# Equal column tiles for the scores, a planner that prices TensorE's tiling, masks on a second engine, and a due time for each attention step

## The chip, the cores and the metric

The kernel runs on one core of one Trainium2 chip. The metric is the device time of one execution in microseconds (us), the median of several runs. The profile is of one execution; its own time is given beside its span below.

The engines in this text: PE is TensorE (matmuls; PEld its weight loads), DVE is VectorE, ACT is ScalarE, POOL is GpSimd, and SP is the engine whose queue issues every DMA of this program.

## The reference

```python
# q, k, v: 4 batches x 8 heads x 768 positions x 64, float32; n_global = 8, n_local = 96
scores = q @ k.T / sqrt(64)
is_global = key < n_global
is_local  = 0 <= query - key < n_local
bias = -slope[head] * distance          # ALiBi; n_local for global keys out of the local window
scores = where(is_global | is_local, scores + bias, -1e9)
a = exp(scores - max);  a = a / (sum(a) + 1e-9);  y = a @ v
x = y, heads side by side               # 3072 tokens x 512
out = ((x @ w_a) * (x @ w_b)) @ w_out   # 512 -> 1536 -> 512
```

So: attention over a window of 96 keys and 8 global ones, and behind it a gated feed-forward layer on the same 3072 tokens. The weights are float64 and reach the device as pairs of 32-bit words.

## The kernel before

**Tiling.** The tokens are cut into six *sequences* u of 512 tokens (four blocks of 128). Names carry the numbers: `ps2_0_1_0` is sequence 2, granule 0, step 1, half 0.

**Attention.** A sequence is four *granules* p; a granule holds four pairs of block and head pair, that is 4 x 128 queries x 2 heads. Its chain:

1. *Scores* (L581, PE, into banks ps): two steps of two blocks each, 48 steps in the program. The array works as four tiles of 64x64: the head (h) picks the rows, the half of the queries (s) picks the columns of the array. A query half needs 168 keys: 96 near ones and 8 global ones, which stand side by side (KX = 104), and 64 more, which lie elsewhere for the lower half (s = 0) and directly behind for the upper half.
2. *Mask* (L602, DVE): one instruction per block and head adds the mask, takes the minimum and writes `t` in SBUF and its row minimum in `sm`. The masks themselves (L514) are made once, one 336-column instruction per head.
3. *Exponential* with row sum (L619, ACT), reciprocal (DVE), *norm* (L658 on ACT or L661 on DVE).
4. *Transposes*: in sequence 0 on PE (`direct`, L749, into banks pt, copied out into px and py); else on DVE (L677, into tt), and through DRAM (`mir`) back into px and py (`carry`, DMAs of SP).
5. *Values* (L701, PE, bank pa): 16 matmuls, then a copy of pa into `X`. In sequences 1 to 3 the values of a granule are emitted after the scores of the next.

**Feed-forward.** The 1536 hidden units are six weight tiles `fp`, each a pair of 128-unit halves for both w_a and w_b and two tiles O0, O1 of w_out. A weight tile is loaded (wr, 512 KB pieces), *converted* from float64 (L369 and L404 on ACT, L376, L384, L394, L411 on DVE) and split into a high and a low part in fp32r, so each product of two numbers takes three matmuls. `STAYS` says which tiles stay for which sequences: tiles 0 to 2 for sequences 0 to 3 with plain products (L943), later stays with a seven-product form (L922). Products go into the banks al and ga, ACT and DVE make h = a * b and its two parts hh and hl, and output matmuls (L1099) add into acc0 to acc3. A stay leaves partial sums in DRAM (part) for the next.

In sequence 0 the tokens are done in two halves of 256, named `(0,)` and `(1,)`: `al0_2_1(1,)` is sequence 0, tile 2, hidden half 1, token half 1.

**What sets the order.** Nothing is reordered on the chip: each engine runs its instructions as written. `Schedule.order` writes them. Every operation is given a due time, a cost on each engine that may do it, and what it reads and writes; the planner simulates the engines with these costs, and whenever one is free it takes, of the operations whose inputs are ready and whose buffers are free, the one that is due first. `wins` decides for operations that two engines may do. The due times come from tables at the head of the file: HALF0, HALF1, STEPS0, QUADS0 to QUADS2 and GAP for sequence 0, SPANS for the attention of sequences 1 to 5 (as positions in the list of passes), CONV for the conversion of tiles. All operations of a granule's chain have one due time, `due`; values and their copy have `due + VLAG`. The core of the planner's choice:

```python
for item in ready[e]:
    op = item[2]
    if e in op.port and port > now:
        continue
    if fits(op) and wins(op, e):
        break
...
free[e] = now + op.costs[e]
```

## Time and profile before

| | before |
|---|---|
| time, median of 3 runs (lowest to highest) | 725.11 us (724.22 to 725.52) |
| the profiled execution: its time, its span | 728.68 us, 726.4 us |
| granted TensorE clock, mean | 0.987 |
| busy in the span: PE, DVE, ACT | 693.5, 578.9, 387.7 us |

The profile is read in stretches: the attention of sequence 0 (7 to 62 us, in which the first weight tiles are converted and the first products begin), its feed-forward (62 to 128 us), sequences 1 to 3 with the first stay (to about 300 us), and the later stays, in which attention of sequences 4 and 5 lies among the products. "PEclk" is the clock that the throttle granted, as a share of full speed. In the rows of the order of time a bracket names the idle time ahead of an instruction on its engine, and what ended it. A row of such a view begins with the start in us and the busy time in us; where rows are grouped, "xcount" and "busy, mean ns" follow. L-numbers are lines of the kernel before; in the rows of the changed kernel the same operations stand some 20 to 26 lines further down (L581 is L607, L602 L628, L619 L645, L701 L727, L943 L969, L1099 L1125, L369 L391, L332 L354).

### The profile page before, as it was taken

The page shows a single profiled execution, that of the slowest core. Times are in us where ns is not written, and L with a number is a line of the kernel's source. Part 1 is how long each engine was busy: PE and PEld are TensorE (multiplying, and loading weights), DVE is VectorE, ACT ScalarE, POOL GpSimd, SP SyncE. Part 2 cuts the span into 40 slices and gives each one's busy share as a digit, 9 for nine tenths or more (in the row PEclk, how much of TensorE's full clock was granted, in tenths as well). Part 3 has the DMA queues.
Part 4 walks back from the last instruction along what each step waited for, and adds up shares of the span by engine and source line. Part 5 has one row for each costly group of instructions (what it writes and reads, how often), then busy time and mean ns, then how long its engine had stood idle before and what let it go on. Part 6 is the DMA issues. An engine that isn't in the chain of part 4 may idle for free.

```text
span 726.4 us, 15134 instructions
## 1 busy us (share of the span) xinstructions
PE 693.5 (95%) x5584; PEld 605.8 (83%) x5584; DVE 578.9 (80%) x1544; ACT 387.7 (53%) x989; POOL 1.8 (0%) x8
## 2 busy tenths in 40 slices
PE   5698998999999999999999999999999999999996
PEld 4487887777777788788899899899989999999995
DVE  7999997777687785799989898999999557746652
ACT  5987775745465673746455545666343434434310
POOL 1000000000000000000000000000000000000000
PEclk9799999999999999999999999999999999999999
DMA  8547998897989897776676888756794423343221
GB/s 296 213 163 259 269 294 300 267 305 250 304 280 303 253 335 247 262 266 228 221 249 232 294 259 301 245 201 230 233 337 151 146 59 102 131 145 102 74 73 62
DMA packets 67906, 162.39 MB, mean 224 GB/s; under 512 B 8432, under 2 KB 21872, under 8 KB 66032
## 3 DMA queue, kind: packets, MB, share of 16 engines
q1 hardware_dynamic: 67824, 161.34, 66.8%
q8 instruction: 46, 0.75, 0.4%
q14 instruction: 36, 0.29, 0.1%
HBM read 110.45 MB, written 50.86 MB: 222 GB/s over the span
## 4 chain that ended last, share of the span: by engine, by line
PE 68%; DMA 12%; DVE 11%; ACT 5%; issue 2%; SPq 1%; DVEq 0%; ACTq 0%
PE acc L1099 19%; PE al L922 16%; PE ga L922 12%; DMA wr<-wts 8%; PE ps L581 4%; PE pa L701 3%; ACT t L619 1%; DMA py<-mir 1%; DVE tt L677 1%; DMA X<-dx 1%; DVE t L602 1%; DVE wm L394 1%; ACT wm L369 1%; DVE wm L411 1%; SPq L323 1%
## 5 line engine op out<-in xcount | busy, mean ns | idle before, releaser
L1099 PE MATMUL acc<-w_O,hh 128*128 128x512 f32 x576 | 196.6, 400 | 0.0
L1099 PEld LDWEIGHTS acc<-w_O,hh 128*128 128x128 f32 x576 | 108.4, 188 | 25.1 <-issue 1.7
L1099 PE MATMUL acc<-w_O,hl 128*128 128x512 f32 x288 | 113.8, 395 | 0.4 <-DVE hl L342 0.3
L619 ACT ACTIVATE t<-t,sm 128x168 f32<-128x168 f32 x192 | 81.1, 424 | 20.2 <-DVE sm L602 20.0
L922 PE MATMUL al<-xf_T,w_S 128*128 128x256 f32 x576 | 76.8, 283 | 0.0
L922 PEld LDWEIGHTS al<-xf_T,w_S 128*128 128x128 f32 x576 | 72.2, 189 | 0.5
L332 ACT CAST hh<-h 128x512 fp32r<-128x512 f32 (+1 forms) x62 | 36.6, 592 | 50.2 <-DVE h L342 22.5
L1099 PEld LDWEIGHTS acc<-w_O,hl 128*128 128x128 f32 x288 | 54.3, 188 | 10.5 <-DVE hl L342 1.1
L581 PEld LDWEIGHTS ps<-qk 64*64 64x64 f32 x1152 | 36.3, 142 | 28.1 <-issue 14.2
L602 DVE CUSTOM_DVE_ANT_0 t<-ps,mask 128x168 f32<-128x168 f32 x192 | 53.3, 326 | 6.1 <-PE ps L581 5.6
L581 PE MATMUL ps<-qk 64*64 64x168 f32 (+2 forms) x1152 | 43.6, 278 | 14.4 <-DMA qk<-qk 7.0
L332 ACT COPY s<-al 128x512 f32<-128x512 f32 x47 | 27.5, 585 | 52.2 <-PE al L922 52.2
L369 ACT ACTIVATE wm<-wr 128x512 f32<-128x512 f32 x54 | 36.2, 670 | 34.7 <-DMA wr<-wts 25.2
L342 DVE TENSOR_TENSOR hl<-h,hh 128x512 fp32r<-128x512 f32 (+1 forms) x78 | 49.8, 642 | 5.2 <-ACT hh L332 4.9
L1031 DVE TENSOR_TENSOR s<-ga,s 128x512 f32<-128x512 f32 x48 | 32.8, 683 | 16.2 <-PE ga L922 16.0
L677 DVE STREAM_TRANSPOSE tt<-t 128x512 f32<-128x512 f32 x80 | 41.1, 552 | 0.8 <-ACT t L658 0.4
L404 ACT ACTIVATE wr<-wr 128x512 int32<-128x512 uint32 x54 | 36.2, 673 | 7.2 <-DMA wr<-wts 4.3
L701 PE MATMUL pa<-px,vt 104*64 104x128 f32 x384 | 38.9, 278 | 1.2 <-DMA px<-mir 1.2
L922 PE MATMUL ga<-xf_B,w_S 128*128 128x256 f32 x288 | 38.6, 283 | 1.3 <-ACT s L332 1.3
L922 PEld LDWEIGHTS al<-xf_B,w_A 128*128 128x128 f32 x288 | 37.5, 189 | 2.3 <-issue 0.3
L922 PE MATMUL ga<-xf_T,w_S 128*128 128x256 f32 x288 | 38.6, 283 | 0.6 <-DVE s L1031 0.5
L701 PE MATMUL pa<-py,vt 128*64 128x128 f32 x384 | 38.0, 273 | 1.1 <-DMA py<-mir 1.0
(274 smaller groups left out, 1318.6 us busy)
## 6 DMA issues: line engine op xcount, KB each, us to landing
wr<-wts SPq DMA_DIRECT2D x54, 512.0 KB
qk<-qk SPq DMA_DIRECT2D x24, 720.0 KB
mir<-tt SPq DMA_DIRECT2D x20, 768.0 KB
vt<-vd SPq DMA_DIRECT2D x24, 512.0 KB
X<-dx SPq DMA_DIRECT2D x10, 1024.0 KB
part<-o SPq DMA_DIRECT2D x32, 256.0 KB
wl_S<-dw_S SPq DMA_DIRECT2D x32, 256.0 KB
px<-mir SPq DMA_DIRECT2D x60, 128.0 KB
```

Source lines behind the costliest of these rows:

```text
L332: self.nc.scalar.copy(out(), src())
L342: lambda e: self.nc.vector.tensor_tensor(out(), a(), b(), op=op),
L369: lambda e: nc.scalar.activation(m(), high().bitcast(F32), AF.Abs),
L404: lambda e: nc.scalar.activation(low(), low().bitcast(U32), AF.Copy, scale=2.0**-29),
L581: nc.tensor.matmul(ps[h][64 * s : 64 * s + 64, c0 + c : c0 + c + w], qk[rows, q0 + 64 * s : q0 + 64 * s + 64], qk[rows, k0 + k : k0 + k + ...
L602: nc.vector.tensor_tensor_reduce(t[:, i, h], b[:, w], self.mask[pair][:, h, kind], -0.125, 3.0e38, ALU.add, ALU.min, sm[:, 0, j : j + 1],)
L619: lambda e, i=i, h=h, j=j: nc.scalar.activation(t[:, i, h], t[:, i, h], AF.Exp, bias=sm[:, 0, j : j + 1], scale=-1.0, accum_out=sm[:, 1, j ...
L677: nc.vector.transpose(dst[:, :, e0 : e0 + n], src[:, :, c0 : c0 + 32 * n].rearrange("p j (e k) -> p j e k", e=n),)
L701: nc.tensor.matmul(pa[64 * h : 64 * h + 64, i * P : i * P + P], vt[:lanes, v0 : v0 + 64], k[:, :, 2 * i + h], start=c == 0, stop=c == 1, s ...
L922: self.nc.tensor.matmul(bank[:, ab * HT : ab * HT + HT], w[:, a, (2 * ab + c) * P : (2 * ab + c) * P + P], x[:, b, c], start=first, stop=F ...
L1031: lambda e: nc.vector.tensor_tensor(s[:, :], bank[:, :], s[:, :], op=ALU.add),
L1099: self.nc.tensor.matmul(acc[i][:, :], a[:, rows], w[:, b], start=first and f == 0 and k == 0, stop=False, skip_group_check=True,)
```

## The change

1. **Score tiles.** Both query halves take their 168 columns as 104 and 64. Before, the upper half took 168 at once. A step goes from 12 to 16 matmuls.
2. **The planner.** An operation on PE can carry a mode; scores and values have mode "t" (tiled). A change of mode is charged SWITCH = 250 ns, and if the operation due first would change it, the planner looks for one of the present mode that is due at most KEEP = 1500 ns later. Costs of scores go from 720 to 620 ns, of values from 1900 to 1760.
3. **Masks** may be made on ACT.
4. **Due times.** Each step of a granule has its own offset: LEAN for sequence 0, LEAN1 for the others (scores, mask, exponential, norm, transposes, values in sequence 0 or the way through DRAM in the others; the seventh of LEAN is the copy into X). Scores are due 2.31 us earlier in sequence 0 and 0.9 us earlier elsewhere; in sequence 0 values are due 5.0 and their copy 5.64 us behind the granule's time.
5. **Tables.** Of the numbers at the head of the file FORM0 (a lead of the first forms of X), LOADLEAD (lead of the loads of q and k), HALF0, HALF1, GAP, one to three entries of STEPS0 and QUADS0 to 2, the end of SPANS[2], the start of SPANS[5] and the start of CONV[5] change.

```diff
-SPANS = {1: (0.0, 0.6), 2: (0.85, 1.6), 3: (1.6, 2.6), 4: (3, 7), 5: (6.79, 11.5)}
+SPANS = {1: (0.0, 0.6), 2: (0.85, 1.3), 3: (1.6, 2.6), 4: (3, 7), 5: (6.7, 11.5)}
-CONV = {3: (1.72, 2.88), 4: (2.5, 3.5), 5: (4.39, 7), 2: (7.27, 10), 0: (10, 12.27), 1: (11.39, 14)}
+CONV = {3: (1.72, 2.88), 4: (2.5, 3.5), 5: (4.14, 7), 2: (7.27, 10), 0: (10, 12.27), 1: (11.39, 14)}
...
+KEEP = 1500.0
+SWITCH = 250.0
+LEAN = (-2310.0, 0.0, 0.0, 0.0, 0.0, 5000.0, 5640.0)
+LEAN1 = (-900.0, 0.0, 0.0, 0.0, 310.0, 0.0)
...
+                    cost = op.costs[e]
+                    if e == "pe":
+                        if op.mode != mode:
+                            for other in ready[e]:
+                                if other[0] > op.due + KEEP:
+                                    break
+                                if other[2].mode == mode and fits(other[2]):
+                                    item, op = other, other[2]
+                                    break
+                        cost = op.costs[e] + (SWITCH if op.mode != mode else 0.0)
+                        mode = op.mode
...
+TILES = [(s, h, 0, 64, KX) for s in range(2) for h in range(2)]
+TILES += [(s, h, KX, (0, KW)[s], 64) for s in range(2) for h in range(2)]
...
+        def scale(e, out, hd):
+            by = self.slope[:, hd : hd + 1]
+            if e == "act":
+                nc.scalar.mul(out, rel(), by)
+            else:
+                nc.vector.tensor_scalar(out, rel(), by, None, op0=ALU.mult)
...
-                    for s, c, k, w in ((1, 0, 64, KW), (0, 0, 64, KX), (0, KX, 0, 64)):
-                        for h in range(2):
...
+                    for s, h, c, k, w in TILES:
...
-            op(due, scores, [qk], ps, pe=720)
+            op(due + lean[0], scores, [qk], ps, pe=620).mode = "t"
```

What the new due times and costs do to the order is seen only in the built programs. Four places follow.

**ACT at the start**, up to the conversion of the first weight pieces. Before:

```order
L1476 TENSOR_LOAD flag_76
L1479 COMPARE_AND_BRANCH
L619 ACT_TABLE_LOAD
L619 ACTIVATE t0_0_160,sm0_0_161<-t0_0_160,sm0_0_161 128x168 x8
L369 ACTIVATE wm0_1_224<-wr0_1_152 128x512
L404 ACTIVATE wr0_1_152<-wr0_1_152 128x512
```

With the change:

```order
L1502 TENSOR_LOAD flag_76
L1505 COMPARE_AND_BRANCH
L535 ACT_TABLE_LOAD
L535 ACTIVATE mask0_162<-X_81,slope_80 128x336
L535 ACTIVATE mask1_165<-X_81,slope_80 128x336
L535 ACTIVATE mask2_172<-X_81,slope_80 128x336
L645 ACTIVATE t0_0_168,sm0_0_169<-t0_0_168,sm0_0_169 128x168 x8
L391 ACTIVATE wm0_1_242<-wr0_1_160 128x512
```

Three masks now stand ahead of the first eight exponentials; DVE makes the other five.

**PE in sequence 0, second token half**, where products fill the banks al and ga. Before:

```order
L943 MATMUL al0_0_1(1,)_900<-xp0_2_458,w0_A22_0_456 128x256 x3
L943 MATMUL al0_0_1(1,)_900<-xp0_3_482,w0_A22_0_456 128x256 x3
L943 MATMUL al0_1_0(0,)_932<-xp0_0_361,w1_A11_0_740 128x256 x3
L943 MATMUL al0_1_0(0,)_932<-xp0_1_372,w1_A11_0_740 128x256 x3
L943 MATMUL al0_1_0(0,)_932<-xp0_2_458,w1_A12_0_773 128x256 x3
L943 MATMUL al0_1_0(0,)_932<-xp0_3_482,w1_A12_0_773 128x256 x3
L943 MATMUL al0_1_1(0,)_959<-xp0_0_361,w1_A21_0_852 128x256 x3
```

With the change:

```order
L969 MATMUL al0_0_1(1,)_950<-xp0_2_481,w0_A22_0_476 128x256 x3
L969 MATMUL al0_0_1(1,)_950<-xp0_3_521,w0_A22_0_476 128x256 x3
L969 MATMUL ga0_0_1(1,)_973<-xp0_0_361,w0_A21_0_443 128x256 x3
L969 MATMUL ga0_0_1(1,)_973<-xp0_1_469,w0_A21_0_443 128x256 x3
L969 MATMUL ga0_0_1(1,)_973<-xp0_2_481,w0_A22_0_476 128x256 x3
L969 MATMUL ga0_0_1(1,)_973<-xp0_3_521,w0_A22_0_476 128x256 x3
L969 MATMUL al0_1_0(0,)_993<-xp0_0_361,w1_A11_0_758 128x256 x3
```

A product into ga now lies between two into al; in all of sequence 0 an al product follows another directly once, and three times before.

**ACT at the end of sequence 0** (wm3: conversion of weight tile 3; X from pa1_3: the copy of the last values of sequence 1; xp1: the forms of X for sequence 1; o0: output sums of sequence 0 on their way out; hh: high parts of h). Before:

```order
L369 ACTIVATE wm3_0_1619<-wr3_0_1582 128x512
L332 CAST xp1_0_1626<-X_81 128x512
L332 CAST xp1_2_1636<-X_81 128x512
L332 COPY o0_0_87371_1644<-acc0_0_704 128x512
L332 COPY o0_1_87371_1650<-acc0_1_713 128x512
L404 ACTIVATE wr3_0_1582<-wr3_0_1582 128x512
L332 COPY o0_2_87371_1667<-acc0_2_1022 128x512
L369 ACTIVATE wm3_1_1692<-wr3_1_1648 128x512
L332 COPY X_81<-pa1_3_1670 128x512
```

With the change:

```order
L354 COPY o0_1_99841_1700<-acc0_1_747 128x512
L426 ACTIVATE wr3_0_1643<-wr3_0_1643 128x512
L354 CAST xp1_0_1710<-X_81 128x512
L354 CAST xp1_2_1718<-X_81 128x512
L354 CAST hh0_2_1_1630<-h0_2_1_1612 128x256
L354 COPY X_81<-pa1_3_1722 128x512
L391 ACTIVATE wm3_1_1752<-wr3_1_1704 128x512
L354 CAST xp1_3_1772<-X_81 128x512
L354 COPY o0_2_99841_1775<-acc0_2_1040 128x512
```

The copy into X stands ahead of the conversion of wr3_1 now, and the form xp1_3 behind it.

**PE at the values of granule 2 of sequence 2** (bank pa2_2). Before:

```order
L943 MATMUL ga1_2_1(0, 1)_2301<-xp1_3_1702,w2_A22_0_1407 128x512 x3
L1099 MATMUL acc1_0_2061<-w1_O0_0_1092,hh1_1_0_1984 128x512
L1099 MATMUL acc1_0_2061<-w1_O0_0_1092,hl1_1_0_1989 128x512
L1099 MATMUL acc1_0_2061<-w1_O0_0_1092,hh1_1_0_1984 128x512
L701 MATMUL pa2_2_2335<-px0_248,vt2_2_2059 64x128 x2
L701 MATMUL pa2_2_2335<-py0_133,vt2_2_2059 64x128 x2
```

With the change:

```order
L969 MATMUL ga1_2_1(0, 1)_2413<-xp1_3_1772,w2_A22_0_1490 128x512 x3
L727 MATMUL pa2_2_2435<-px0_261,vt2_2_2148 64x128 x2
L727 MATMUL pa2_2_2435<-py0_137,vt2_2_2148 64x128 x2
L727 MATMUL pa2_2_2435<-px0_261,vt2_2_2148 64x128 x2
L727 MATMUL pa2_2_2435<-py0_137,vt2_2_2148 64x128 x2
L727 MATMUL pa2_2_2435<-px0_261,vt2_2_2148 64x128 x2
```

Three output matmuls into acc1_0, which stood ahead of these values, now stand behind them.

On DVE, in sequences 1 to 3, conversions of weights come earlier and attention's transposes later than before. The runs of tiled matmuls on PE, between products and output matmuls, number 63 before and 64 with the change.

More of the change, by code (lines that the diff above doesn't have):

```diff
@@ L83 @@
 AHEAD = 0.5
-FORM0 = 2410.0
+FORM0 = 3520.0
 START = 25980.0
-LOADLEAD = 7790.0
+LOADLEAD = 8130.0
 VLAG = 13280.0
@@ L174, in op @@
         self.ops.append(Op(len(self.ops), due, costs, emit, reads, writes, late, port))
+        return self.ops[-1]
     def order(self):
@@ L185, in order @@
         port = 0.0
+        mode = None
         def arrive(op):
@@ L240, in order @@
                     out.append(op)
-                    free[e] = now + op.costs[e]
+                    free[e] = now + cost
                     if e in op.port:
@@ L513, in masks @@
                 -1e5 + hd if p < 2 else 4000.0 + hd,
-                lambda e, p=p, h=h, hd=hd: nc.vector.tensor_scalar(
-                    self.mask[p][:, h].rearrange("p a b -> p (a b)"),
-                    rel(),
-                    self.slope[:, hd : hd + 1],
-                    None,
-                    op0=ALU.mult,
+                lambda e, p=p, h=h, hd=hd: scale(
+                    e, self.mask[p][:, h].rearrange("p a b -> p (a b)"), hd
                 ),
@@ L524, in masks @@
                 dve=dve(n, True),
+                act=act(n),
             )
@@ L680, in turn @@
                     )
-            op(due, turn, ts, [(tt, half)], dve=dve(512) + dve(256))
+            op(due + lean[4], turn, ts, [(tt, half)], dve=dve(512) + dve(256))
         if u not in DIRECT:
-            self.carry(n, due, tt, px, py)
+            self.carry(n, due + lean[5], tt, px, py)
         def late():
-            self.values(u, p, due, vt, px, py, x, d)
+            self.values(u, p, due + (VLAG if u else lean[5]), vt, px, py, x, d)
         return late
@@ L713, in values @@
         pr += [(py, ("b", i, s)) for i in range(NH) for s in range(2)]
-        op(due + VLAG, values, [vt] + pr, [pa], pe=1900)
+        op(due, values, [vt] + pr, [pa], pe=1760).mode = "t"
         if d is None:
@@ L717, in values @@
                 self.copy(
-                    due + VLAG, lambda: x[:, p], lambda: pa[:, :], T, [pa], halves(x, p), psum=True
+                    due, lambda: x[:, p], lambda: pa[:, :], T, [pa], halves(x, p), psum=True
                 )
@@ L731, in values @@
             return
-        self.copy(due + VLAG, lambda: vt[:, :T], lambda: pa[:, :], T, [pa], [vt], psum=True)
+        self.copy(due, lambda: vt[:, :T], lambda: pa[:, :], T, [pa], [vt], psum=True)
         self.dma(
-            due + VLAG,
+            due,
             lambda: d[:, p * T : p * T + T],
```

50 lines of the change are left out of this document (26 added, 24 removed).

## The prediction

> **What bounds the kernel now.** I read the page's first lines, then the busy times by stretch (each row: the stretch, its length, each engine's busy time, the granted clock, the DMA share), then the chain and the order of time where PE stands idle.
>
> ```profile
> span 726.4 us, 15134 instructions
> PE 693.5 (95%) x5584; PEld 605.8 (83%) x5584; DVE 578.9 (80%) x1544; ACT 387.7 (53%) x989; POOL 1.8 (0%) x8
> ...
> core 0: us, PE busy (x) PEld busy (x) DVE busy (x) ACT busy (x) POOL busy (x), PEclk, DMA share, GB/s
> 0.00:7.00 7.00, 0.00 (x0) 0.00 (x0) 2.33 (x11) 1.28 (x1) 1.83 (x8) 1.00 0.61 196
> 7.00:20.00 13.00, 10.94 (x168) 9.42 (x168) 12.93 (x62) 9.79 (x36) 0.00 (x0) 1.00 0.87 315
> 20.00:38.00 18.00, 11.45 (x121) 9.35 (x116) 17.48 (x72) 17.36 (x63) 0.00 (x0) 0.73 0.57 215
> 38.00:62.00 24.00, 20.60 (x223) 17.72 (x222) 22.57 (x80) 20.30 (x63) 0.00 (x0) 0.93 0.63 212
> 62.00:118.00 56.00, 54.24 (x530) 48.35 (x530) 52.12 (x173) 39.40 (x113) 0.00 (x0) 0.99 0.85 269
> 118.00:128.00 10.00, 8.02 (x71) 6.02 (x70) 6.70 (x22) 4.58 (x13) 0.00 (x0) 0.83 0.96 343
> 128.00:300.00 172.00, 170.12 (x1296) 133.84 (x1295) 126.46 (x383) 99.18 (x274) 0.00 (x0) 1.00 0.85 283
> 300.00:550.00 250.00, 248.00 (x2041) 224.02 (x2040) 231.50 (x554) 137.96 (x329) 0.00 (x0) 1.00 0.75 250
> ```
>
> PE bounds the program. Its idle time is 32.9 us: 7.0 before the first scores, 12.0 from 7 to 62 us, 1.8 to 118, 2.0 to 128, 1.9 to 300, 2.0 to 550, and 6.2 behind that, almost all at the end. From 7 to 62 us it is DVE that has no time left (53.0 of 55 us), and PE waits for it. So the change can gain little after 62 us, 7.6 us of idle time at the very most, unless PE's own work shrinks.
>
> **Masks on ScalarE.** DVE made four masks before the first scores could be read; now two of them and one later one stand on ACT.
>
> ```profile
> 8.44 1.31 DVE L514 TENSOR_SCALAR mask<-X,slope 128x336 f32<-128x336 f32 x4
> 9.66 0.33 DVE L602 CUSTOM_DVE_ANT_0 t<-ps,mask 128x168 f32<-128x168 f32 x1
> 10.03 0.43 ACT L619 ACTIVATE t<-t,sm 128x168 f32<-128x168 f32 x1 [3.11 <-DVE sm L602]
> 23.64 0.42 PE L749 MATMUL pt<-ident,t 128*104 128x128 f32 x1 [3.47 <-DVE t L661]
> ```
>
> Four masks took 9.66 - 8.44 = 1.22 us, 0.30 each, so three are worth 0.9 us of DVE. ACT was idle for 3.11 us there, which hides them: a 336-column operation on ACT is not in the trace; between its 168 columns (0.43) and, without a limit from above, twice that (0.86), three end between 9.8 and 11.1 us, and the first exponential moves by -0.2 to +1.1 us. I take 0.45 each, nearest the lower row. Behind this, two granules' exponentials and norms keep their order, and PE's 3.47 us wait at 23.64 stays, about 0.5 us sooner. In return the plan puts five evictions of transposes more on DVE by 45 us, and the forms that gate the first product come no sooner. Price: -0.4, between -0.9 and +0.5.
>
> **Products alternate between the banks.** In sequence 0 each half-product (12 matmuls of 256 columns) fills bank al or ga. Three times one al product follows another directly and waits for ACT to copy the bank out.
>
> ```profile
> 64.88 1.68 PE L943 MATMUL al_1(1,)_900<-xp,w_A 128*128 128x256 f32 x12
> 67.02 1.68 PE L943 MATMUL al_0(0,)_932<-xp,w_A 128*128 128x256 f32 x12 [0.46 <-ACT s_1(1,)_918 L332]
> 69.20 1.69 PE L943 MATMUL al_1(0,)_959<-xp,w_A 128*128 128x256 f32 x12 [0.50 <-ACT s_0(0,)_955 L332]
> ...
> 102.68 1.59 PE L943 MATMUL ga_1(0,)_1461<-xp,w_A 128*128 128x256 f32 x12
> 104.10 1.58 PE L943 MATMUL al_0(1,)_1489<-xp,w_A 128*128 128x256 f32 x12
> 106.14 1.69 PE L943 MATMUL al_1(1,)_1524<-xp,w_A 128*128 128x256 f32 x12 [0.46 <-ACT s_0(1,)_1519 L332]
> ```
>
> Without a wait starts lie 104.10 - 102.68 = 1.42 apart; with it 2.14, 2.18 and 2.04, so 0.6 to 0.8 us each. The new order has one such pair (al0_1_1 before al0_1_0 of the other half). Two fewer: -1.4, between 0 (something later is the limit) and -2.1.
>
> **The end of sequence 0.** Before, the copy of the last values (X) stands on ACT behind a weight conversion whose DMA is late; the scores behind it on PE wait for the bank.
>
> ```profile
> 119.31 0.44 PE L701 MATMUL pa<-py,vt 128*64 128x128 f32 x4 [0.24 <-DMA py<-mir]
> 121.00 0.50 PE L581 MATMUL ps<-qk 64*64 64x168 f32 x2
> 123.24 0.81 PE L581 MATMUL ps<-qk 64*64 64x168 f32 x22 [1.74 <-ACT X L332]
> ...
> 122.05 0.66 ACT L369 ACTIVATE wm<-wr 128x512 f32<-128x512 f32 x1 [3.42 <-DMA wr<-wts]
> 122.61 0.57 ACT L332 COPY X<-pa 128x512 f32<-128x512 f32 x1
> ...
> 124.05 4.55 PE al_0(0, 1)_1726 L943 x12
> 139.80 2.80 PE al_0(0, 1)_1899 L943 x12
> 583.95 5.60 PE acc L1099 x24
> ...
> 177.58 0.44 PE L701 MATMUL pa<-px,vt 104*64 104x128 f32 x4 [1.16 <-DMA px<-mir]
> ```
>
> The new order has the copy ahead of the conversion, so the scores no longer wait: 123.24 - 121.00 = 2.2 us. It also moves two groups of three output matmuls (6 of 5.60 / 24 = 0.23 us, 1.4 us) behind the values; that much PE then waits in front of them, since the values are held by the DMA of py anyway (119.31). Net 0.8 us. One form, xp1_3, is still cast behind the conversion; its product starts with the other three, which take 2.1 us, and I cost it at nothing. If the weight DMA comes over 2 us later, al1_0_0 stalls instead. Then the clock: behind the 2.2 us wait the next product took 4.55 us against 2.80 for an equal one, and PEclk reads 0.83 there, while after the wait of 1.16 at 177.58 the stretch's PEclk stays at 1.00. With the wait cut to some 1.4 us, most of those 1.75 us should return: I take 1.4. Together -2.2, between 0 and -3.9 (2.2 + 1.75). The Trainium skill ("TensorE: Matmul & The Clock Gate", Part 1) says that the array goes to half clock after an idle window of about 3.4 us; by it this 2.2 us gap would have cost no clock, and the term would be 0.8. The trace differs, so its rows decide.
>
> **The values of granule 2, sequence 2.** At 177.58 they already wait for the way through DRAM. The new order puts three output matmuls behind them that stood ahead: 3 x 0.23 = +0.7, between 0 (the DMA comes sooner) and +1.5 (it comes that much later).
>
> **Tilings and matmuls.** The plan now charges 250 ns for a change of tiling and looks for an equal one, yet the built order has 64 runs of tiled matmuls, 63 before.
>
> ```profile
> 150.12 2.99 PE ga_1(0, 1)_2017 L943 x12
> ...
> 153.04 0.82 PE L581 MATMUL ps<-qk 64*64 64x168 f32 x24
> 153.79 0.50 PE L1099 MATMUL acc<-w_O,hh 128*128 128x512 f32 x1
> ...
> L1099 PE MATMUL acc<-w_O,hh 128*128 128x512 f32 x576 | 196.6, 400 | 0.0
> ```
>
> A product before a run takes 2.99 instead of 2.80, and the first matmul behind it 0.50 instead of its group's mean of 0.40: 0.3 us a run, so +0.3 (0 to 0.6). Each of the 48 scores steps goes from 12 to 16 matmuls, 24 to 32 records. The streamed columns stay. Lower tile columns already did 104 + 64, the upper ones 168, side by side, and the step took 153.79 - 153.04 = 0.75 for the longer of the two; with both as 104 + 64 I take 0. Bounds: -0.5 in all (10 ns a step), and from above the records in proportion, 0.25 us a step, 12 us.
>
> **The rest**, dues of attention and of the conversion of tiles 4 and 5, moves work among DVE, ACT and SP from 128 to 550 us, where PE idles 3.9 us in all: I take 0, between -2 and the loss below. The last 164 us before 714 keep their order of products.
>
> **Sum:** -0.4 - 1.4 - 2.2 + 0.7 + 0.3 = -3.0. The profiled execution took 728.68 us (2.28 outside the span), 3.57 over the median of 725.11; 728.68 less 3.0 is 725.68, and that less 3.57 is 722.1.
>
> **Rivals.** *Conversions ahead of attention.* In sequences 1 to 3 the new DVE order does weight conversions earlier and attention's transposes later. Ahead of the transposes of granule 1, sequence 3, stand one more piece of a tile's conversion (four operations) and the four combining operations of tile 4, each the size of L394's.
>
> ```profile
> L394 DVE SCALAR_TENSOR_TENSOR wm<-wr,wm 128x512 int32<-128x512 int32 x54 | 36.9, 684 | 0.7
> L411 DVE CUSTOM_DVE_ANT_0 wm<-wr,wm 128x1024 uint16<-128x1024 uint16 x54 | 36.8, 682 | 0.8
> ...
> L384 DVE TENSOR_SCALAR wm<-wm 128x512 int32<-128x512 int32 x54 | 22.7, 420 | 0.5
> L376 DVE TENSOR_SCALAR wm<-wm 128x512 f32<-128x512 f32 x54 | 22.5, 417 | 15.0 <-ACT wm L369 12.6 <-DMA py<-mir 2.4
> ...
> 250.18 1.71 SPq L323 DMA_DIRECT2D py<-mir  x4
> ...
> 254.09 0.44 PE L701 MATMUL pa<-px,vt 104*64 104x128 f32 x4
> ```
>
> A piece is 0.68 + 0.68 + 0.42 + 0.42 = 2.2 us, the four others 4 x 0.68 = 2.7: 4.9 us more ahead. DVE idles 45 us from 128 to 300, which should take this in. But the way from transpose to values has no slack: the last load of granule 3, sequence 3, is issued by 251.9, and PE starts those values 2.2 us later. If the idle time lies elsewhere, the 4.9 us become waits of PE in front of values: 722.1 + 4.9 = 727.0. It turns slower once they come over 4.5 us late. *Small matmuls cost.* If a record held its tile quarter for the mean 0.75 / 24 = 31 ns beside its columns, the four more records of the upper quarters would make 0.125 us a step, 6.0 in all: 728.1. Against it: the halves with more records set no longer time that I can see. The Trainium skill ("TensorEngine Tiling (Array Packing)", Instruction Overhead) states about 60 cycles for each matmul; by it, 25 ns, it would be 4.8 us and 726.9. *The gains turn into waits.* DVE and DMA (85% busy from 62 to 118) hand over at the same time as before, PE reaches the values of sequence 1 earlier and waits longer there, the clock falls again: only -0.4 + 0.7 + 0.3 stay, and -0.8: 724.9. *The charge does nothing* is already counted: the runs are not fewer.
>
> **Numbers.** My forecast 0.50 (719 to 724), gains turned into waits 0.22, conversions ahead 0.20, small matmuls 0.08. A change under 0.2% (1.45 us) is about what a measurement of this kernel cannot tell from none. Faster, below 723.66: nearly all of the first and little of the second, 0.52; within: 0.25; slower: 0.23. The range goes from all lower bounds of the three gains (-6.9, less 0.7 and 0.3 of loss, and 1.7 of the 3.9 us idle behind 128 us: 725.1 - 7.6 = 717.5) to the dearest rival, 728.5.
>
> **What the profile after would show.** First exponential by 10.2 us; one al product with a wait for ACT between 60 and 110 us instead of three; the scores of sequence 2 without a wait for X, and the first product of the second pass at 2.8 to 3 us; a wait of 2 us at the values of granule 2; scores steps still 0.75 us. Wrong would make it: scores steps over 0.78, waits for px or py over 2 us in sequences 2 and 3, or ACT held at a weight DMA with a form behind it.

## The result, and the profile after

The changed kernel took 733.39 us in the median of 4 runs (730.75 to 737.24), the kernel before 725.32 in 4 runs beside them: a ratio of 1.0115, with a 95% interval from 1.0075 to 1.0156. It is slower, by about 8 us. The profiled execution took 731.67 us.

The first lines of its profile, and the busy times by stretch:

```profile
span 730.2 us, 15911 instructions
PE 693.6 (95%) x5968; PEld 605.2 (83%) x5968; DVE 576.4 (79%) x1546; ACT 389.5 (53%) x987; POOL 1.8 (0%) x8
...
62.00:118.00 56.00, 53.64 (x590) 47.80 (x590) 50.86 (x170) 38.58 (x109) 0.00 (x0) 1.00 0.88 279
118.00:128.00 10.00, 9.85 (x111) 7.42 (x106) 9.58 (x35) 7.41 (x23) 0.00 (x0) 1.00 0.98 311
128.00:300.00 172.00, 169.30 (x1431) 132.84 (x1430) 131.80 (x402) 97.22 (x263) 0.00 (x0) 1.00 0.88 291
300.00:550.00 250.00, 243.52 (x2086) 220.02 (x2086) 221.39 (x529) 136.50 (x323) 0.00 (x0) 1.00 0.74 244
```

The 384 more instructions of PE are the 48 x 8 more records of the scores. PE is as busy as before (693.6 against 693.5 us). From 118 to 128 us it now idles 0.15 us instead of 2.0; from 128 to 300 it idles 2.7 instead of 1.9, and from 300 to 550 6.5 instead of 2.0.

The profiled execution before was 3.6 us over the median. The better yardstick is a control that ran later: the order and tiles of before, put out from a list, in a program that is the same instruction by instruction. Its traced execution took 723.59 us:

```profile
span 721.4 us, 15134 instructions
...
128.00:300.00 172.00, 171.82 (x1304) 135.40 (x1303) 130.66 (x398) 104.00 (x290) 0.00 (x0) 1.00 0.87 286
300.00:550.00 250.00, 248.95 (x2040) 226.26 (x2040) 231.73 (x548) 135.11 (x317) 0.00 (x0) 1.00 0.75 250
```

There PE idles 0.2 and 1.05 us, 1.2 from 128 to 550 us; the changed kernel idles 9.2 in the same stretches. These 8.0 us come near the difference of the two spans (8.8), but only because the rest nearly cancels: up to 128 us the changed kernel idles 3.8 us less than the control, behind 550 us 0.6 more, and PE is busy 4.0 us longer in all (693.6 against 689.6). What PE waited for there, first in the changed kernel from 128 to 300 us and from 300 to 550 (us in total, times, longest):

```profile
PE pa L727 <- DMA px<-mir: 1.1, 2, 0.8
PE pa L727 <- DMA py<-mir: 0.9, 2, 0.5
PE ps L607 <- ACT X L354: 0.4, 1, 0.4
...
PE ga L948 <- DVE s L1057: 2.2, 3, 1.8
PE ga L948 <- ACT s L354: 1.3, 1, 1.3
PE pa L727 <- DMA px<-mir: 1.3, 1, 1.3
PE pa L727 <- DMA py<-mir: 0.8, 1, 0.8
PE al L948 <- ACT s L354: 0.8, 1, 0.8
```

Values that wait for their way through DRAM (px, py) make 4.1 us, products that wait until DVE or ACT has read their bank out (s) 4.3, scores that wait for X 0.4. In the control the same view has one wait of 0.2 from 128 to 300 and three, 0.8 together, behind that. The second kind shows in the order of time how a queue passes a delay on (DVE, the changed kernel; then the product that waits, on PE):

```profile
545.94 0.69 DVE L1160 TENSOR_TENSOR o<-acc,o 128x512 f32<-128x512 f32 x1 [1.26 <-DMA o<-part]
546.55 0.42 DVE L356 CAST xf_B<-X 128x512 fp32r<-128x512 f32 x1
547.00 0.69 DVE L364 TENSOR_TENSOR xf_B<-X,xf_B 128x512 fp32r<-128x512 f32 x1
548.34 0.69 DVE L1160 TENSOR_TENSOR o<-acc,o 128x512 f32<-128x512 f32 x1 [0.65 <-DMA o<-part]
548.95 0.68 DVE L1057 TENSOR_TENSOR s<-ga,s 128x512 f32<-128x512 f32 x1
...
549.69 1.69 PE L948 MATMUL ga<-xf_T,w_S 128*128 128x256 f32 x12 [1.82 <-DVE s L1057]
```

DVE stands twice, 1.91 us, at a sum whose partial result has not come back from DRAM (part); the addition that reads ga, and so frees the bank, stands behind both in its queue, and PE waits 1.82 us for it. PE's wait is put down to DVE; its origin is a load.

Start of the same work in five traces (the fourth product of sequence 1, which is its second into ga; the first product of tile 3; and the span, in us):

| | sequence 1's fourth product | tile 3's first product | span |
|---|---|---|---|
| before | 136.75 | 291.56 | 726.4 |
| control | 134.67 | 287.48 | 721.4 |
| after | 132.82 | 289.57 | 730.2 |
| after again | 133.92 | 291.80 | 729.8 |
| after's order, old tiles | 135.79 | 294.59 | 734.7 |

Against the trace of before the change was 3.9 us ahead at the first mark. It then lost 1.9 us to the second, and 5.8 more to the end. Against the control the lead is 1.85, and the losses are 3.9 and 6.7.

### The profile page after: what moved, and what is told of

It reads as the page before. It is cut to its first block, busy times and chain, and to the rows that moved or that the text cites. A ratio compares the mean times of both kernels' runs of the same rounds, so it can differ in the third digit from the quotient of the medians.

```text
span 730.2 us, 15911 instructions
## 1 busy us (share of the span) xinstructions
PE 693.6 (95%) x5968; PEld 605.2 (83%) x5968; DVE 576.4 (79%) x1546; ACT 389.5 (53%) x987; POOL 1.8 (0%) x8
## 4 chain that ended last, share of the span: by engine, by line
PE 50%; DVE 21%; DMA 21%; ACT 5%; issue 2%; SPq 1%; DVEq 0%; ACTq 0%
PE acc L1125 15%; PE al L948 12%; PE ga L948 9%; DMA wr<-wts 8%; PE pa L727 3%; DVE t L628 2%; PE ps L607 2%; DMA X<-dx 2%; DMA wl_S<-dw_S 2%; DMA out<-o 1%; DVE tt L703 1%; DMA py<-mir 1%; DVE wm L433 1%; DMA mir<-tt 1%; ACT t L645 1%
## 5 line engine op out<-in xcount | busy, mean ns | idle before, releaser
L607 PE MATMUL ps<-qk 64*64 64x64 f32 (+1 forms) x1536 | 44.3, 253 | 10.5 <-DMA qk<-qk 7.3
L398 DVE TENSOR_SCALAR wm<-wm 128x512 f32<-128x512 f32 x54 | 22.5, 418 | 33.5 <-ACT wm L391 33.4
L1057 DVE TENSOR_TENSOR s<-ga,s 128x512 f32<-128x512 f32 x48 | 32.9, 685 | 15.7 <-PE ga L948 15.6
```

Source lines behind the costliest of these rows:

```text
L607: nc.tensor.matmul(ps[h][64 * s : 64 * s + 64, c0 + c : c0 + c + w], qk[rows, q0 + 64 * s : q0 + 64 * s + 64], qk[rows, k0 + k : k0 + k + ...
L1057: lambda e: nc.vector.tensor_tensor(s[:, :], bank[:, :], s[:, :], op=ALU.add),
```

## The experiments

Each is timed in 5 rounds against the kernel before on the same chip; a ratio's interval is 95%. Lines in their rows differ by kernel; the operations are the same. "Put out by list" means that the planner is bypassed:

```diff
-        order, end = self.plan.order()
+        order = self.plan.listed(ORDER)
```

ORDER gives every operation's place and engine, so that an order and the tiles can be combined freely.

**Theory at the start.** The new order costs time behind 300 us, in the later stays, because ACT and DVE are held there at DMAs. *Rivals:* conversions stand ahead of attention in sequences 1 to 3; the tiles with more records cost it.

### Tiles, front and back of the order

New tiles with before's order; with after's order up to the first product of tile 3 and before's behind it; the reverse; and the changed kernel again.

> The order of before on every engine, word for word, but the score steps with the new tiles (104 and 64 for both halves). Theory 'order behind 300 us' (the loss comes from ACT and DVE being held at DMAs in the stays behind pass 4): no change, 724 to 726.5 us. Rival 'small matmuls cost' (each scores step longer by its four more matmuls): 727 to 731, and scores steps of 0.85 us or more instead of 0.75.

> The order of after up to the first product of tile 3 for sequence 3 (near 290 us), everything left behind it in the order of before; new tiles throughout. Theory 'order behind 300 us': the gain that the trace of after shows at 290 us (2.0 us) stays, so 721.5 to 724.5 us, and the waits at 356, 444 and 547 us are gone. Rival 'conversions ahead of attention' (sequences 1 to 3): 727 to 732. Rival 'small matmuls cost': 728 or more, since 32 of 48 steps lie in this part.

> The order of before up to the first product of tile 3 for sequence 3, everything left in the order of after; new tiles throughout. Theory 'order behind 300 us': all of the loss and none of the gain, 730 to 737 us, PE idle time from 300 to 550 us of 5 us or more (2.0 before). Rival 'conversions ahead of attention' in sequences 1 to 3: 725 to 727.

> The changed kernel itself, once more on the chip of the three others. All theories: 731 to 736 us. Theory 'order behind 300 us': whatever differs between its executions lies behind 300 us in the trace, as waits of ACT or DVE for DMAs.

Measured: tiles alone 1.0083 (1.0050 to 1.0116); front new 1.0074 (1.0042 to 1.0106); back new 1.0282 (1.0241 to 1.0323); after again 1.0145 (1.0112 to 1.0177). The tiles alone cost, against my theory, 0.8%. Back new has a fault of its own: the seam, where the two orders meet, leaves a product waiting for 8.1 us for ACT's copy, so the run says nothing on the back. With the seam's wait taken off it is about 1.017, no better than after. After's order up to 290 us costs nothing beyond the tiles, so of the change's loss the 3 to 5 us by which it is slower than front new arise behind 290 us. That front new costs nothing more is a balance, though: in its trace it reaches sequence 1 earlier than tiles alone and loses 3.0 us more from there to tile 3 (its row in the table further down). The gain at 290 us that the theory counted on did not show in its time.

### Order alone, control, more records, no charge

```diff
-TILES = [(s, h, 0, 64, KX) for s in range(2) for h in range(2)]
-TILES += [(s, h, KX, (0, KW)[s], 64) for s in range(2) for h in range(2)]
+TILES = [(s, h, 52 * j, 64 + 52 * j, 52) for j in range(2) for s in range(2) for h in range(2)]
+TILES += [
+    (s, h, KX + 32 * j, (0, KW)[s] + 32 * j, 32)
+    for j in range(2)
+    for s in range(2)
+    for h in range(2)
+]
```

The diff is that of the halved tiles (32 matmuls a step, before's order). Without a charge means, in the changed kernel, SWITCH and KEEP 0 and the old costs 720 and 1900, with its tiles, masks and due times.

> The order of after on every engine, masks on ACT included, with the score tiles of before (12 matmuls a step). If tiles and order each cost their own (731.0 for the tiles alone, 735.7 for both, against 726.1): 729 to 732 us, that is +0.4 to +0.8%. If the +0.83% of the tiles alone was an accident of its load and the order carries all: 734 to 737. If the tiles carry all and the order nothing: 725 to 727.

> The order of before and the score tiles of before, instruction for instruction, only put out by the machinery of the experiments (an order written as a list). Every theory: the time of before, ratio within 0.2% of 1. If it comes out 0.5% or more off, equal programs differ by the accident of where they lie, and the +0.83% of the tiles alone proves nothing.

> The order of before, with each column tile of the scores cut in two: 32 matmuls a step (52 and 32 columns) instead of 16 or 12, the same streamed columns. 'A price for each small matmul' that the first trace of the new tiles doesn't show in its steps (0.75 us in both): five times as many more matmuls as the new tiles have, so +20 us or more, 745 to 755. 'A price of another kind, or none' (steps stay at 0.75 us): 725 to 732. If the array takes time for each record: steps of 1.0 us or more.

> The changed kernel with the planner of before: no charge for a change of tiling, no look-ahead, scores at 720 and values at 1900 ns again; new tiles, due times and masks stay. Theory 'the charge shifts ACT's and DVE's work against PE behind 300 us': the loss of the order goes and that of the tiles stays, 729.5 to 732 us, PE idle for 3.5 us or less from 300 to 550 us. Rival 'the new due times of attention do it' (SPANS and LEAN1): 734 to 737.

Measured: after's order with the old tiles 1.0126 (1.0088 to 1.0164), the control 0.9993 (0.9961 to 1.0024), halved tiles 1.0203 (1.0158 to 1.0248), no charge 1.0103 (1.0073 to 1.0132). So the order alone gives the whole loss, and on top of it the tiles cost nothing that shows (1.0115 and 1.0145 with them), though on before's order they cost 0.8%. The parts don't add.

A scores step (PE) of the changed kernel, and of the halved tiles:

```profile
120.14 0.82 PE L607 MATMUL ps<-qk 64*64 64x104 f32 x32
120.89 0.50 PE L1125 MATMUL acc<-w_O,hh 128*128 128x512 f32 x1
```

```profile
158.15 1.14 PE L818 MATMUL ps<-qk 64*64 64x52 f32 x64
159.22 0.50 PE L1336 MATMUL acc<-w_O,hh 128*128 128x512 f32 x1
```

From start to start it is 0.75 us with 32 records, as with 24, and 1.07 with 64. So up to 32 records their number does not set the step's length here; at 64 it does, with 0.92 us from the first start to the last, 14.5 ns each. 48 steps x 0.317 = 15.2 us is the loss of the halved tiles (15.6). The longer step is thus not how the new tiles cost their 6 us.

Without the charge the time, 733.8, lies between the two expectations. In its trace the kernel was 7 us behind the control at sequence 1's fourth product, lost some 4 more to tile 3's first product, and nothing behind it.

### Conversions put back

322 operations of conversion stand in after's order, behind sequence 0, where before's order has them against PE; the reverse with the old tiles; and only tiles 3 and 4 put back (106 operations).

> The order of after, with one class of work put back to where before has it against PE's work: the conversion of weight tiles behind sequence 0 (from tile 3 on: loads wr, the steps on ACT and DVE, the writes to DRAM), 322 operations. PE's order stays that of after, word for word, and so do all else. Theory 'conversions stand at the head of DVE's and ACT's queues before their weights have come': 726 to 729 us, DVE's wait for the first step of a conversion from 128 to 300 us under 10 us (24 to 28 us in the orders of after, 5 to 7 in those of before). Rival 'the moved attention (due times, SPANS) costs it': 733 to 736.

> The reverse: the order and the score tiles of before, with the same 322 operations put where after has them against PE's work. Theory 'conversions at the head of the queues': 730 to 735 us, DVE's wait for the first step of a conversion from 128 to 300 us over 15 us. Rival 'moved attention': 724 to 727.

> As the first of these, but only the conversions of tiles 3 and 4 are put back (106 operations, all near sequences 1 to 3); those of tiles 5, 2, 0 and 1 stay as early as in after. Theory 'conversions at the head of the queues': the loss between 135 and 291 us goes (3.5 to 5 us), that behind 291 us stays, 729 to 732 us. Rival 'moved attention': 733 to 736.

Measured: 1.0702 (1.0657 to 1.0747), 1.1241 (1.1206 to 1.1277), 1.0508 (1.0465 to 1.0552). All three miss by far. Putting the conversions back took most of DVE's wait at their first step away (DVE, 128 to 300 us; the changed kernel, then the first of these):

```profile
DVE wm L398 <- ACT wm L391: 24.9, 11, 7.4
```

```profile
DVE wm L604 <- ACT wm L597: 6.5, 5, 1.6
```

and cost 41 us more all the same. The likely reason, which no run separates, is that the rest of the order was planned around the conversions as they were. These runs show how dear a misplaced queue is, up to 90 us; they don't show what the conversions' places in the changed kernel cost.

### Parts of the planner, and the front alone

Tiles again; the charge alone (before with SWITCH 250, KEEP 1500 and costs 620 and 1760; old tiles, masks and tables); after's order up to sequence 1's first product, 122 us, then before's, old tiles; and a test of where the stream of PE's instructions falls, described further down.

> The order of before with the new score tiles, once more. Its first timing gave +0.83%, while its trace shows each step at 0.75 us as before, and the order of after costs the same with old and new tiles. If the tiles cost time that no trace shows: 729 to 733 us. If that was an accident of its load: 724 to 727.

> Before with one part of the change: the planner's charge for a change of tiling, its look-ahead and the new costs of scores and values. Score tiles, masks, due times and all tables are those of before. Theory 'the charge alone makes the order that costs': 730 to 736 us, stretches from the fourth product of sequence 1 to tile 3's first product (135 to 291 us) and from there to 558 us longer by 2 to 5 us each. Rival 'due times and tables do it': 724 to 727.

> The order of after up to the first product of sequence 1 (near 122 us), all else in the order of before, score tiles of before. This holds the prediction's three gains (masks on ACT, alternating banks, the copy into X ahead of a conversion) without what follows. If they are real and kept: 721.5 to 724 us. If they are lost in later waits: 724.5 to 728.

Measured: tiles again 1.0085 (1.0055 to 1.0115); charge alone 1.0210 (1.0168 to 1.0252); after's sequence 0 alone 0.9990 (0.9970 to 1.0011). The charge alone is worse than the whole change, and above the 730 to 736 us expected. The front alone, which holds all the gains that I forecast, is worth -0.7 us (-2.2 to +0.8). It is as fast as before, and it is the only new order that lost nothing. What the charge alone makes PE wait for, from 128 to 300 us:

```profile
PE pa L726 <- DMA px<-mir: 1.3, 1, 1.3
PE pa L726 <- DMA py<-mir: 1.1, 3, 0.6
PE ps L606 <- DVE sm L627: 0.9, 2, 0.5
```

Values that come late, and scores whose bank DVE has not read.

### Is it the size of the charge, or the due times?

> As the charge alone (old tiles, masks and tables), but a change of tiling is charged 150 ns instead of 250. In its plan the weight conversions stand near where before has them against PE's work (1 to 2 PE operations earlier on average), while with 250 they stand 4, 10 and 35 earlier in the stretches of sequence 1, of sequences 2 and 3 and behind them; attention stays within one operation. Theory 'conversions come ahead into the queues of DVE and ACT, because the plan takes PE for slower than it is': 726 to 732 us, DVE's wait for the first step of a conversion from 128 to 300 us under 10 us. Rival 'the look-ahead and the grouping of tiled steps cost it': 735 to 742.

> Before with the other parts: masks that may be made on ACT, due times of each attention step, all new tables; the planner's costs and the score tiles are those of before. Theory 'the charge made the loss': 724.5 to 728.5 us. Rival 'due times and tables cost their own, in sequence 0 above all' (the kernel without the charge but with new tiles lost 6 us there): 729 to 735.

Measured: a charge of 150 gives 1.0151 (1.0103 to 1.0199); the tables, due times and masks alone, with the old planner and tiles, 1.0096 (1.0062 to 1.0130). With 150 the conversions no longer stand early in the order, yet values wait just as long (px 1.5, py 1.1 us from 128 to 300), and DVE's wait at their first step is 24.3 us. So "conversions stand ahead because the plan takes PE for slower" falls, by its own expectation; 735.9 us lies in the rival's range (the look-ahead and the grouping of tiled steps). The due times alone were 7 us behind the control at sequence 1's fourth product and lost 3 more to tile 3, much as the change without the charge did, and little behind that.

The larger part of those 7 us is PE's clock. From 7 us to that product PE was busy for 114.9 us with the due times alone, for 115.7 without the charge, and for 110.8 in the control, at granted clocks of 0.91, 0.92 and 0.97. The busy times by stretch, the due times alone, then the control:

```profile
7.00:62.00 55.00, 42.18 (x468) 34.33 (x468) 48.57 (x185) 46.47 (x150) 0.00 (x0) 0.84 0.62 208
62.00:118.00 56.00, 49.26 (x503) 44.71 (x504) 51.38 (x186) 36.41 (x112) 0.00 (x0) 0.94 0.86 268
```

```profile
7.00:62.00 55.00, 42.39 (x509) 35.74 (x510) 52.54 (x212) 46.76 (x157) 0.00 (x0) 0.94 0.69 234
62.00:118.00 56.00, 53.82 (x526) 47.36 (x524) 52.33 (x172) 39.23 (x115) 0.00 (x0) 1.00 0.88 271
```

It is no accident of two traces: the mean granted clock was 0.978 to 0.987 in all 18 executions of these two kernels (median 0.983), and 0.985 to 0.994 in the 79 of the kernel before that ran beside the experiments (median 0.991). The difference of 0.8% of 725 us, 6 us, is an estimate from above of what the clock cost, since a low clock costs nothing while PE idles.

What each trace has, beside the timed ratio: the start of sequence 1's fourth product, the time from there to tile 3's first product and from there to one same product late in the program (558 us in the trace of before), and PE's idle time in the two stretches, read as in the rows shown:

| | fourth product | to tile 3 | to the late one | idle 128-300 | idle 300-550 | ratio |
|---|---|---|---|---|---|---|
| control | 134.7 | 152.8 | 265.3 | 0.2 | 1.0 | 0.9993 |
| after's sequence 0, then before's | 131.5 | 152.5 | 265.0 | 0.0 | 1.4 | 0.9990 |
| tiles alone | 135.6 | 153.8 | 265.5 | 0.8 | 1.9 | 1.0083 |
| tiles again | 139.6 | 153.8 | 270.3 | 0.9 | 4.9 | 1.0085 |
| due times, tables, masks | 141.4 | 155.8 | 265.9 | 1.9 | 1.0 | 1.0096 |
| after without the charge | 141.6 | 156.9 | 264.4 | 1.9 | 1.1 | 1.0103 |
| charge alone | 138.3 | 158.7 | 267.5 | 3.3 | 2.3 | 1.0210 |
| charge of 150 alone | 142.2 | 158.9 | 269.5 | 3.5 | 3.0 | 1.0151 |
| after's order to tile 3, then before's, new tiles | 133.9 | 156.8 | 267.8 | 2.6 | 3.1 | 1.0074 |
| after's order, old tiles | 135.8 | 158.8 | 270.8 | 3.6 | 4.5 | 1.0126 |
| after | 132.8 | 156.8 | 271.5 | 2.7 | 6.5 | 1.0115 |
| after again | 133.9 | 157.9 | 269.0 | 3.2 | 3.5 | 1.0145 |

All orders planned with a charge idle 2.6 to 3.6 us in the first stretch, 1.2 to 2.6 of it in front of values. Those of the table without it idle at most 1.9, with 0 to 0.7 in front of values; in the two with new due times 1.5 and 1.8 is one wait for X. (In the trace of before the 1.9 us are all in front of values, so late values are not the charge's alone. The shifted new tiles of the next section, without a charge, idle 2.5, one wait for X.) The charge alone and after's order lose much the same to tile 3, 4 to 6 us against the control, and 2 to 6 behind it. Idle time is about half of what they lose to tile 3: for the same matmuls between the two marks PE is busy for 152.6 us in the control, for 155.2 with after's order and the old tiles, and for 155.9 with the charge alone.

### Where PE's instruction stream falls

In the two traces of the new tiles on before's order one wait stands out: PE waits 1.5 and 1.7 us for a copy of ACT, which stands behind a conversion that waits 5.4 and 5.5 us for its weights. The same load in the control takes 3.3 us from issue to landing. In the load's time there is one more packet in the slow case, of the queue by which PE's instructions come (packets, MB, share of the 16 DMA engines from issue to landing; tiles again, then the control):

```profile
q1 hardware_dynamic: 815, 1.26, 92.5%
q8 instruction: 1, 0.02, 1.4%
```

```profile
q1 hardware_dynamic: 419, 0.92, 78.6%
```

*Theory:* a fetch of instructions holds up one of the load's DMA engines; more matmuls move the places where fetches fall. *Rival:* the tile shape itself. To tell them apart, 32 small matmuls (256 instructions are one 16,384-byte packet) stand ahead of the first scores, with old and with new tiles, in before's order:

```diff
+for _ in range(32 if u + p + r == 0 else 0):
+    nc.tensor.matmul(ps[0][:64, :8], self.ident[:64, :64], self.ident[:64, :8], ...)
```

> The order and the score tiles of before, with 32 matmuls of 8 columns (their result is overwritten) ahead of the first scores, where PE waits for its first data. They move every later instruction of PE by 128 records against the 16 KB pieces in which they are fetched. If the new tiles cost time by shifting that stream against the other transfers: a change of over 2 us either way, under 723 or over 728. If not: 724.5 to 727.5.

> The same 32 matmuls with the order of before and the new score tiles, to be read against the kernel with the new tiles alone (731.0 and 732.2). If the +6 us of the new tiles come from where the fetches of PE's instructions fall: 724 to 729 us. If they come from the tiles themselves: 730 to 734.

Measured: 1.0132 (1.0092 to 1.0173) and 1.0155 (1.0125 to 1.0185). As times they are of little use: the small matmuls began at 5.76 us, took 6.67, and the first scores came at 12.2 instead of 7.0. The first product of the second token half, at 60 us, stood 3.9 and 5.7 us later than in the control and in tiles again, so this late start is some half of the loss with the old tiles (7.5 us), and with the new ones more than all by which they are slower than tiles again (4.0 us). The load in question answers the theory, by ACT's rows at its conversion in the control, in tiles again, with the old tiles shifted, and with the new tiles shifted:

```profile
394.46 0.69 ACT L632 ACTIVATE wr<-wr 128x512 int32<-128x512 uint32 x1 [3.21 <-DMA wr<-wts]
```

```profile
403.20 0.65 ACT L632 ACTIVATE wr<-wr 128x512 int32<-128x512 uint32 x1 [5.49 <-DMA wr<-wts]
403.76 0.57 ACT L560 COPY s<-al 128x512 f32<-128x512 f32 x1
...
404.38 0.85 PE L1154 MATMUL al<-xf_T,w_S 128*128 128x256 f32 x5 [1.69 <-ACT s L560]
```

```profile
402.55 0.65 ACT L632 ACTIVATE wr<-wr 128x512 int32<-128x512 uint32 x1 [5.02 <-DMA wr<-wts]
```

```profile
404.56 0.68 ACT L632 ACTIVATE wr<-wr 128x512 int32<-128x512 uint32 x1 [3.43 <-DMA wr<-wts]
```

The shift turns it round: the old tiles now have a fetch in the load's time, and PE waits 1.2 us; the new tiles have none, and PE waits for nothing there. In eight traces this load took 3.2 to 3.3 us without a fetch and 5.0 to 5.3 with one, and the fetch began 1.0 to 1.5 us behind the load's issue, so it isn't there only because the load took long. So the shape is not the cause here; its count of instructions is, by chance of position. Over some 40 loads that met both cases in different traces the difference is 0.4 to 0.5 us in the mean, so this one is an extreme. It explains 1.5 to 1.7 of the tiles' 6 us; where the others go is open.

## Why the prediction was wrong

Forecast were 722.1 us (717.5 to 728.5); measured 733.4. The step that failed is "The rest": "moves work among DVE, ACT and SP from 128 to 550 us, where PE idles 3.9 us in all: I take 0, between -2 and the loss below". That bounded what could be won by the idle time there, but took as price of a new order the one delay that I had named. (The dearest rival named comes to 728.1; the upper bound of 728.5 is no rival's sum.) Measured, the stretch from sequence 1 to tile 3 lost 1.9 us against the trace of before and 3.9 against the control, and the stretch behind 4.9 and 6.2 to 558 us.

Step by step:

- **Masks on ScalarE.** The mechanism came: the first exponential starts at 9.85 instead of 10.03, and three masks end on ACT in 1.51 us (0.5 each; taken 0.45).

```profile
8.43 1.51 ACT L535 ACTIVATE mask<-X,slope 128x336 f32<-128x336 f32 x3 [1.43 <-DVE X L529]
9.85 0.42 ACT L645 ACTIVATE t<-t,sm 128x168 f32<-128x168 f32 x1
...
118.94 0.59 ACT L354 COPY X<-pa 128x512 f32<-128x512 f32 x1 [0.95 <-PE pa L727]
119.71 0.67 ACT L391 ACTIVATE wm<-wr 128x512 f32<-128x512 f32 x1 [0.19 <-DMA wr<-wts]
```

- **Banks in turn.** One al product waits for ACT (0.60 us, at 75.75) instead of three, as forecast.
- **The end of sequence 0.** The last two rows above are the copy of X ahead of the conversion, and the conversion's load came almost in time, so nothing stalled behind it. The scores on PE have no wait (the row at 120.14 above), and the product behind them takes 2.96 us instead of 4.55:

```profile
75.75 1.68 PE L969 MATMUL al_0(1,)_1133<-xp,w_A 128*128 128x256 f32 x12 [0.60 <-ACT s_1(0,)_1125 L354]
...
121.69 2.96 PE L969 MATMUL al_0(0, 1)_1787<-xp,w_A 128*128 128x512 f32 x12
...
182.46 0.44 PE L727 MATMUL pa<-px,vt 104*64 104x128 f32 x4 [0.77 <-DMA px<-mir]
183.32 0.44 PE L727 MATMUL pa<-py,vt 128*64 128x128 f32 x4 [0.41 <-DMA py<-mir]
```

- The sum of these three, -4.0, is what the trace shows at 135 us against that of before (-3.9). But that trace was no fair base. In the control the same scores wait 1.34 us, and the product behind them takes 3.06:

```profile
122.70 0.81 PE L813 MATMUL ps<-qk 64*64 64x168 f32 x22 [1.34 <-ACT X L560]
123.44 3.06 PE L1175 MATMUL al_0(0, 1)_1726<-xp,w_A 128*128 128x512 f32 x12
```

  The clock term of -1.4 belonged to one execution. The Trainium skill ("TensorE: Matmul & The Clock Gate", Part 1) calls the window behind the gate free-running and its effect different from run to run; these two traces agree in that, with a loss of 1.75 us behind 1.74 us of idle time in the one (granted clock 0.83 from 118 to 128 us), and next to none behind 1.34 in the other (1.00; 3.06 us against 2.96 where nothing waited). In timed runs after's sequence 0 alone is worth -0.7 us (-2.2 to +0.8), not -4. Taking 3.57 us off for the base's distance from the median, and counting as a gain what had made it long, counted the same microseconds twice.
- **Values of granule 2, sequence 2.** The last two rows of the fence on PE: 0.77 + 0.41 = 1.2 us of wait. Before had 1.16 for px and, in the row behind it, 0.37 for py, 1.5 in all. So neither the price of 0.7 nor the forecast wait of 2 us came; the wait was 0.35 us shorter, a little below the lower bound of 0.

```profile
178.39 0.44 PE L701 MATMUL pa<-py,vt 128*64 128x128 f32 x4 [0.37 <-DMA py<-mir]
```

- **Tilings and matmuls.** Steps stayed at 0.75 us, as taken. The rival with the small matmuls gave 6.0 us for them, and tiles alone cost 6; but its way, longer steps, isn't what happened, and on the new order the cost is gone: that the numbers agree is luck.
- **Conversions ahead of attention** was the rival nearest to the truth: values do wait for px and py, 4.1 us in all where it had 4.9. It was sized on one granule, left the products' waits for their banks out (4.3 us), and named a cause, the conversions' places, that the experiments did not bear out.
- **Signs of being wrong.** Steps stayed at 0.75 us, and the waits for px and py from 128 to 300 us came to 2.0, only just the named bound. No sign was named for banks that are freed late, which is where 4.3 us went.
- **Gains turn to waits** foresaw waits in front of values too, but at 724.9 it held that nothing would be lost beyond the gains.

Shown: the loss comes with the order behind 122 us (after's sequence 0 with before's order behind it loses nothing; after's whole order with the old tiles loses it all), and the charge alone brings more than all of it. In the traces the loss lies in PE's waits for values and for banks and, to a smaller part, in a longer busy time for the same matmuls. Not shown: that the charge is the only source. The change without it still took 1.0103 (1.0073 to 1.0132), which overlaps the change's own 1.0115 (1.0075 to 1.0156); its loss lies ahead of tile 3, the larger part of it in sequence 0, where the clock was low, and not behind. Not shown either: which moved operations start the waits. DVE's wait at the first step of a conversion from 128 to 300 us goes along with the charge in after's orders (24.1 to 27.7 us, control 4.9), but 24.1 is that of after's order up to tile 3, which costs nothing beyond its tiles, it is 12.7 in the charge alone, which is slower still, and the kernel that took most of it away lost more elsewhere. A plan with the charge in which the conversions alone keep before's places, and all else is planned around them, was not tried.

One correction to the text ahead: in LEAN the 5.64 us of the copy into X come on top of the 5.0 of the values.

## What to carry to other kernels

An order that leaves its first engine 1 to 4 us of idle time in 420 fits the times at which loads really land. A re-plan of it should not be priced at zero: count, for each queue that changes, what stands behind the instruction that waits for a DMA, and take a loss as the likelier sign. Read the granted clock beside the idle time: two of the orders here lost 7 us ahead of 141 us, the larger part of it to a lower clock. One profile holds accidents of its execution; a gain read from it should be looked for in a second trace of the same program before it goes into a sum. And parts of such a change are not to be added: here 0.8% (tiles), 1.0% (due times, tables, masks) and 2.1% (charge) made 1.2 to 1.5% together.

## What the runs showed of the hardware

PE's instructions themselves come by DMA, in packets of 16,384 bytes, through the same 16 engines as the weights. The page counts them (changed kernel; packets, MB, share):

```profile
q8 instruction: 49, 0.80, 0.4%
```

It is 46 before and 61 with the halved tiles; the change has 384 matmuls and 384 weight loads more than before, 768 instructions, and 3 packets. A packet holds an engine for about 1 us (1.4% of 16 engines' 5.2 us in the fence on tiles again). The Trainium skill ("Runtime: NRT & Kernel Launch", Instruction fetch mechanics) has the same size, 256 instructions, and calls the cost mostly hidden. For PE itself no run here shows otherwise; but a weight load beside a fetch landed 0.4 to 0.5 us later in the mean and some 2 us later in the one case above, where PE waited for it (1.2 to 1.7 us).

Executions of one program differ more than the interval of a median suggests: the kernel before took 719 to 731 us over all runs, and the traced execution of tiles alone was the fastest of its seven, 725.0, with a median of 731.0. Single traces were therefore read for mechanisms here, and timed rounds for sizes.
